# A fused Nyström attention, softplus block and expert layer: w_out blocks decoded in attention, product banks moved, one mixture unit issued in one piece

## The chip, the cores and the metric

The kernel runs on one core of a Trainium2 chip. The metric is the device time of one execution in microseconds (us); the median of three runs stands for a kernel. Engines are called TensorE (PE in the profile, PEld for its weight loads), VectorE (DVE), ScalarE (ACT), GpSimd (POOL) and SyncE (SP, which issues most of the DMAs). TensorE's clock has two levels, 1.2 and 2.4 GHz; the profile shows the granted one as a share of the higher.

## What is computed

Three stages follow one another. `w_in` and `w_out` come in as 64-bit floats, the other inputs and the results are float32.

```python
def _attn_ref(q, k, v):                      # (4, 8, 576, 64) each, 32 landmarks
    A  = sm(q, k_lm); Bm = sm(q_lm, k_lm); C = sm(q_lm, k)
    Z  = Bm.T / (norm1(Bm) * norminf(Bm) + 1e-06)
    for _ in range(6):
        Z = 2 * Z - Z @ Bm @ Z               # pseudo-inverse
    return A @ Z @ C @ v

def _moe_ref(x, w_in, w_out):                # x (2304, 512), w_in (512, 2048), w_out (2048, 512)
    h = x @ w_in
    g = np.maximum(h, 0.0) + np.log1p(np.exp(-np.abs(h)))
    return g @ w_out

def _moe2_ref(x, w_gate, w_output_gate, w1, w2):   # 8 experts, one per token
    ...
```

## The kernel before

Each product in the second and third stage is made of three matmuls on high and low halves: a float32 operand is split into `hi` (rounded) and `lo` (the rest), and hi·hi, hi·lo and lo·hi are added up in a bank of PSUM.

Attention is written as a list of steps, `PLAN`, which a scheduler may interleave on each engine. K, V are loads, T transposes, M landmarks, A and C scores, N the pseudo-inverse (tile tag `sm0`, `sm1` of pool `psm`), E the product with v, F the last product of a batch (tile `ps_x` of pool `pss`, copied by ScalarE to `xo`, line 379). `W i` decodes block i of w_in and `O` decodes block 0 of w_out, while attention runs: a load on SP, `decode_f64` (ScalarE's Abs at line 96, then three VectorE operations at lines 97, 99 and 101 that put the bits together), and `split_hi_lo` (ScalarE copies `hi`, GpSimd subtracts `lo`). The plan has W0 to W9 and one O. `X` prepares the first chunk of x, `x0`.

The mixture (the second stage) goes over 9 chunks of 256 tokens and 8 pairs p of 128-column blocks. One unit is `gemm1(p, x)` (24 matmuls, line 618, into a bank `ps_h`), softplus on ScalarE and VectorE (two halves `gh`, `gl`), and `gemm2` (12 matmuls, line 657, into two banks `acc` of its chunk). Chunks 0 to 2 run jointly, pair by pair, in units 0 to 23, because w_in and w_out are still being decoded; chunks 3 to 8 follow in units 24 to 71. `gemm2` of a unit stands two units behind its `gemm1` (`LAG = 2`). `ps_h` has two banks; units 2 and 3 borrow `acc2` and `tr`. The order on every engine in this stage is the order of the text (`tc.manual_schedule()`).

`weights()` decodes what attention has not: 15 blocks of w_out and 6 of w_in, a list of 21 jobs sorted by when they are due, in four steps each, with VectorE subtracting `lo`. Raw blocks have three buffers, and `load_w(n + 3)` issues a load when block n is decoded. `units(n)` takes n steps. Twelve steps, three jobs, stand ahead of the loop; then each unit takes `U = 1, 1, 2` steps at three places. Softplus of a unit is cut in three pieces, `softplus_a` in its own turn, `softplus_b` and `softplus_c` in the next:

```python
                if i - 1 in ga:
                    gs[i - 1] = softplus_b(*ga.pop(i - 1))
                ...
                    h = gemm1(p, xs[c], *HB.get(i, ()))
                    units(u[0])
                    sp_ = softplus_a(h)
                    next(sp_)
                    if i - 1 in gs:
                        gs[i - 1] = softplus_c(gs[i - 1])
                    ga[i] = next(sp_)
                    units(u[1])
```

`split_x` splits a later chunk's x, at unit 23 for chunk 3. `gate` and `early` make the routing of a finished chunk in small steps (`next(side)`) between the products, two per unit and four in the last chunk (`hook`). The third stage (`run_slots`) keeps the transposed hidden tiles `hh`, `hlo` in pool `e3`, three deep.

Of the kernel before, what the change touches and what calls it, by code (L numbers as in the profile page):

```python
# [1 line left out]

# [27 lines left out]
CH = 256  # L30
# [9 lines left out]
N1 X0 V5 M6 C4 T6 C5 C6 E4 M7 V6 V7 N2 A5 E5 W0 F1 N3 W1 W2 E6 W3 T7 A6 W4 O0 C7 A7 W5 F2 W6 E7 W7 F3 W8 W9  # L40
"""
NWA = 10
# [5 lines left out]
U = 1, 1, 2  # L48
# [38 lines left out]
def decode_f64(nc, pool, src, shape, tag="dect", **kw):  # L87
# [28 lines left out]
def moe_nystrom_kernel(ctx: ExitStack, tc: tile.TileContext, q, k, v, w_in, w_out, w_gate, w_ogate, w1, w2,  # L116
# [23 lines left out]
    wo0 = [x0_pool.tile([128, DM], F32R, name=n) for n in ("wo0h", "wo0l")]  # L140


    with ExitStack() as actx:
# [267 lines left out]
        def prep_wo0():  # L411
            raw = ld.tile([128, 2 * DM], I32, tag="q", name="raw")
            nc.sync.dma_start(raw, w_out.bitcast(I32)[:128, :])
            a = list(decode_f64(nc, a3, raw.unsqueeze(1), [128, 1, DM], bufs=2))[-1]
            split_hi_lo(nc, a[:, 0], wo0[0], wo0[1], nc.gpsimd)
# [12 lines left out]
            "O": lambda _: prep_wo0(),  # L428
# [115 lines left out]
    with ExitStack() as mctx:  # L544
# [9 lines left out]
        woh = [wo0[0]] + [wo.tile([128, DM], F32R, name=f"woh{f}") for f in range(1, NFF)]  # L554
        wol = [wo0[1]] + [wo.tile([128, DM], F32R, name=f"wol{f}") for f in range(1, NFF)]

        due = [(3 * (f // 2) + 2 * (f == 1), "o", f) for f in range(1, NFF)]
# [14 lines left out]
        def weights():  # L572

            for n, (kind, f) in enumerate(jobs):
                for a in decode_f64(nc, m2, raws.pop(n).unsqueeze(1), [128, 1, DM], tag="x2t"):
                    if a is None:
                        yield
                load_w(n + 3)
                yield
                a = a[:, 0]  # L580
                if kind == "o":
                    split_hi_lo(nc, a, woh[f], wol[f], nc.vector)
                else:
                    split_hi_lo(nc, a.rearrange("p (k f) -> p k f", k=4), wcols(whi, f), wcols(wlo, f), nc.vector)
                yield
# [38 lines left out]
        def softplus_a(h):  # L624
            t = sp.tile([128, 2, CH], F32, tag="t", name="t")
            u = sp.tile([128, 2, CH], F32, tag="u", name="u")
            l = sp.tile([128, 2, CH], F32, tag="l", name="l")
            nc.scalar.activation(t, h, AF.Abs)  # L628
            nc.scalar.activation(t, t, AF.Exp, scale=-1.0)  # L629
            nc.scalar.activation(u, t, AF.Identity, bias=1.0)  # L630
            yield
            nc.scalar.activation(l, t, AF.Ln, bias=1.0)  # L632
            nc.vector.scalar_tensor_tensor(u, u, -1.0, t, ALU.add, ALU.subtract)  # L633
            yield h, u, l

        def softplus_b(h, u, l):

            d = sp.tile([128, 2, CH], F32, tag="d", name="d")
            nc.vector.scalar_tensor_tensor(d, h, 0.0, u, ALU.max, ALU.subtract)  # L639
            nc.vector.tensor_tensor(l, l, d, ALU.add)  # L640
            return l

        def softplus_c(l):
            gh = m3.tile([128, 2, CH], F32R, tag="gh", name="gh")
            gl = m3.tile([128, 2, CH], F32R, tag="gl", name="gl")
# [194 lines left out]
        with tc.manual_schedule():  # L840
# [3 lines left out]
            for nm, src in ((0, w_gate), (1, w_ogate)):  # L844
                nc.sync.dma_start(wg[:, :, nm * NE:(nm + 1) * NE], src.rearrange("(k p) e -> p k e", p=128))
# [31 lines left out]
            for i in range(len(order) + LAG):  # L877
# [12 lines left out]
                if i - 1 in ga:  # L890
                    gs[i - 1] = softplus_b(*ga.pop(i - 1))
# [195 lines left out]
```

## Time and profile before

| | |
|---|---|
| median of 3 runs | 920.24 us (918.68 to 920.66) |
| the profiled execution | 920.92 us, of which 919.1 are the span of the trace |
| TensorE busy | 863.8 us, 94% |
| VectorE, ScalarE, GpSimd busy | 72%, 64%, 23% |
| mean granted clock of TensorE | 0.982 |

Attention ends near 150 us, the joint units end near 303, chunks 3 to 8 near 602, and the experts take the rest. A line of a timeline gives the start, the duration, engine, line, operation, the tile written and those read, the count of merged instructions, and in brackets how long the engine stood idle before it and what released it. A line of a table by stage gives, for a stretch, the busy time of each engine with its count of instructions, the granted clock and the share of time in which DMA engines were busy. Busy times of overlapping matmuls merge into one, and the distance of two starts says more than a duration.

### The profile page before, as it was taken

To read this page: it belongs to the slowest core of one execution; us is meant where nothing else is said; L and a number is where in the kernel's file an instruction comes from. 1 tells how busy PE (TensorE), PEld (TensorE's weight loads), DVE (VectorE), ACT (ScalarE), POOL (GpSimd) and SP (SyncE) were. 2 spreads that over 40 slices of the span, in tenths; PEclk is the share of its full clock that TensorE was granted. 3 is DMA by queue.
4 is the path that set the end of the run, shared out by engine and by line. 5 is a ranking of instruction groups with operands and counts; after the bars stand their busy time and mean duration, and the time that the engine had idled before them with its cause. 6 is when DMAs were issued, how large, how long until landed. Compare 5 with 4: busy or idle time off the path is not lost.

```text
span 919.1 us, 15441 instructions
## 1 busy us (share of the span) xinstructions
PE 863.8 (94%) x5826; PEld 717.5 (78%) x5826; DVE 660.8 (72%) x1121; ACT 589.2 (64%) x958; POOL 209.6 (23%) x109
## 2 busy tenths in 40 slices
PE   6998987599999999999999999998999999999996
PEld 3665655478788899999999998886878888888885
DVE  0846697787775546665546464668899999999994
ACT  2554564666666655555555555464888888888893
POOL 0001132000000000000000000024666677666662
PEclk9999997799999999999999999999999999999998
DMA  9856466323210000100111000141117459531600
GB/s 228 188 137 182 146 189 194 94 89 92 82 46 13 24 1 24 46 22 4 46 46 47 1 24 1 47 184 47 44 37 264 174 182 378 184 126 34 225 31 33
DMA packets 49516, 90.93 MB, mean 99 GB/s; under 512 B 5471, under 2 KB 32095, under 8 KB 47392
## 3 DMA queue, kind: packets, MB, share of 16 engines
q1 hardware_dynamic: 41408, 74.43, 26.1%
q0 software_dynamic: 3680, 10.78, 3.6%
q10 hardware_dynamic: 4352, 4.72, 1.5%
q8 instruction: 47, 0.77, 0.4%
q14 instruction: 29, 0.24, 0.1%
HBM read 134.46 MB, written 15.48 MB: 163 GB/s over the span
## 4 chain that ended last, share of the span: by engine, by line
PE 68%; DVE 13%; ACT 10%; issue 4%; DMA 4%; POOL 0%; SPq 0%; POOLq 0%; ACTq 0%; DVEq 0%
PE ps_h L618 16%; PE acc L657 14%; PE ps_g L956 12%; PE ps_y L982 11%; DVE dect L99 2%; DVE deca L101 2%; PE ps_hT L970 2%; PE ps_lg L682 2%; ACT t L629 2%; ACT u L630 2%; ACT deca L96 2%; ACT gh L646 1%; DVE u L633 1%; PE ps_t L184 1%; PE ps_t L160 1%
## 5 line engine op out<-in xcount | busy, mean ns | idle before, releaser
L478 DVE TENSOR_TENSOR lo<-raw,hi 128x1024 fp32r<-128x1024 f32 x129 | 228.7, 1799 | 8.8 <-ACT hi L476 8.6
L476 ACT ACTIVATE hi<-raw 128x1024 fp32r<-128x1024 f32 x176 | 176.8, 1063 | 8.4 <-DMA raw<-in_moe_w 8.3
L618 PE MATMUL ps_h<-xh,whi 128*128 128x256 f32 x512 | 147.4, 288 | 5.8 <-DVE d L639 4.1
L618 PE MATMUL ps_h<-xl,whi 128*128 128x256 f32 x512 | 144.9, 283 | 0.3 <-DVE xl L107 0.3
L618 PE MATMUL ps_h<-xh,wlo 128*128 128x256 f32 x512 | 144.8, 283 | 0.0
L647 DVE TENSOR_TENSOR gl<-l,gh 128x512 fp32r<-128x512 f32 x72 | 49.9, 692 | 129.0 <-ACT gh L646 129.0
L485 POOL DMA_INDIRECT xg<-x_d,gidx x23 | 37.8, 1645 | 452.4 <-ACT t L628 441.4
L478 POOL TENSOR_TENSOR lo<-raw,hi 128x1024 fp32r<-128x1024 f32 x47 | 115.9, 2468 | 35.3 <-ACT hi L476 35.2
L618 PEld LDWEIGHTS ps_h<-xh,whi 128*128 128x128 f32 x512 | 98.0, 191 | 11.4 <-DVE d L639 7.9
L618 PEld LDWEIGHTS ps_h<-xl,whi 128*128 128x128 f32 x512 | 98.0, 191 | 1.9 <-DVE xl L107 0.5
L618 PEld LDWEIGHTS ps_h<-xh,wlo 128*128 128x128 f32 x512 | 97.9, 191 | 0.0
L657 PE MATMUL acc<-woh,gh 128*128 128x512 f32 x240 | 96.2, 401 | 0.0
L657 PE MATMUL acc<-wol,gh 128*128 128x512 f32 x240 | 94.5, 394 | 0.0
L657 PE MATMUL acc<-woh,gl 128*128 128x512 f32 x240 | 94.3, 393 | 0.0
L628 ACT ACTIVATE t<-ps_h 128x512 f32<-128x512 f32 x72 | 42.6, 592 | 69.6 <-PE ps_h L618 50.0
L632 ACT ACTIVATE l<-t 128x512 f32<-128x512 f32 x72 | 45.5, 632 | 55.1 <-DVE gl L647 55.1
L982 PE MATMUL ps_y<-hi,hh 128*128 128x512 f32 x184 | 76.7, 417 | 0.2 <-ACT hh L974 0.2
L982 PE MATMUL ps_y<-hi,hlo 128*128 128x512 f32 x184 | 73.3, 398 | 1.7 <-DVE hlo L975 1.6
L956 PE MATMUL ps_g<-hi,x0l 128*128 128x512 f32 x184 | 73.9, 402 | 0.1
L982 PE MATMUL ps_y<-lo,hh 128*128 128x512 f32 x184 | 72.7, 395 | 0.0
L956 PE MATMUL ps_g<-hi,x0h 128*128 128x512 f32 x184 | 72.0, 391 | 0.0
L956 PE MATMUL ps_g<-lo,x0h 128*128 128x512 f32 x184 | 71.9, 391 | 0.0
(263 smaller groups left out, 1790.4 us busy)
## 6 DMA issues: line engine op xcount, KB each, us to landing
raw<-in_moe_w SPq DMA_DIRECT2D x88, 1024.0 KB
raw<-in_moe_w_in SPq DMA_DIRECT2D x16, 512.0 KB
raw<-in_moe_w_out SPq DMA_DIRECT2D x16, 512.0 KB
x_d<-x SPq DMA_DIRECT2D x9, 514.0 KB
k<-in_k SPq DMA_DIRECT2D x8, 576.0 KB
q<-in_q SPq DMA_DIRECT2D x8, 576.0 KB
v<-in_v SPq DMA_DIRECT2D x8, 576.0 KB
xT_d<-xo ACTq DMA_DIRECT2D x16, 288.0 KB
```

The source lines that it names most:

```text
L96: nc.scalar.activation(a, hi32.bitcast(F32), AF.Abs, scale=2.0 ** -112)
L99: nc.vector.scalar_tensor_tensor(t, hi32, -0x80000000, t, ALU.bitwise_and, ALU.bitwise_or)
L476: nc.scalar.activation(w[0][:, us], raw[i][:, us], AF.Copy)
L478: eng.tensor_tensor(w[1][:, us], raw[i][:, us], w[0][:, us].bitcast(F32), ALU.subtract)
L485: nc.gpsimd.indirect_dma_start(out=xg, out_offset=None, in_=src, in_offset=bass.IndirectOffsetOnAxis(ap=gidx[:, s:s + 1], axis=0))
L618: nc.tensor.matmul(ps[:, i], a[:, kk], b_[:, kk], start=n == 0, stop=n == 11)
L628: nc.scalar.activation(t, h, AF.Abs)
L632: nc.scalar.activation(l, t, AF.Ln, bias=1.0)
L647: nc.vector.tensor_tensor(gl, l, gh.bitcast(F32), ALU.subtract)
L657: nc.tensor.matmul(acc[tt], a[:, i, ts_], b_[f], start=f == 0 and n == 0, stop=f == NFF - 1 and n == 2)
L956: nc.tensor.matmul(ps, a[:, kk], b_[:, kk], start=n == 0, stop=n == 11)
L982: nc.tensor.matmul(y, a[:, kk], b_[:, kk], start=half == 0 and n == 0, stop=half == 1 and n == 11)
```

## The change

`O` becomes a step with an argument: O0, O1 and O2 decode blocks 0 to 2 of w_out in attention, and W8 and W9 are dropped from the plan, so that blocks 8 to 15 of w_in are decoded in the mixture. `units(12)` ahead of the loop is gone; unit 0 takes no weight step inside its softplus. `weights()` works one job ahead: ScalarE's Abs of the next block is issued with the `hi` copy of this one, then `lo`, then the three VectorE operations of the next block; three steps per job, one job per unit, and a further job after units 5 and 8 (`EXTRA`). A unit's softplus is issued in one piece in its own turn. Setting up the routing constants and loading the gate weights moves from ahead of the loop to behind unit 2. Pool `psm` is created ahead of `pss`, so that `ps_h`, which takes the third and fourth bank, lies where `psm` was. In the last stage `hh` and `hlo` cycle through the space of the three w_out blocks.

```diff
-... W5 F2 W6 E7 W7 F3 W8 W9
+... W5 F2 W6 O1 E7 W7 F3 O2
-NWA = 10
+NWA = 8
+NWO = 3
+EXTRA = 0, 5, 8
-U = 1, 1, 2
...
     nc.scalar.activation(a, hi32.bitcast(F32), AF.Abs, scale=2.0 ** -112)
+    yield
     nc.vector.tensor_scalar(t, a.bitcast(I32), 3, None, ALU.logical_shift_left)
-    yield
     nc.vector.scalar_tensor_tensor(t, hi32, -0x80000000, t, ALU.bitwise_and, ALU.bitwise_or)
-    yield
     nc.vector.scalar_tensor_tensor(a.bitcast(I32), lo32, 29, t, ALU.logical_shift_right, ALU.bitwise_or)
...
+        psm = actx.enter_context(tc.tile_pool(name="psm", bufs=1, space=PSUM))
         pss = actx.enter_context(tc.tile_pool(name="pss", bufs=2, space=PSUM))
-        psm = actx.enter_context(tc.tile_pool(name="psm", bufs=1, space=PSUM))
...
-        def prep_wo0():
+        def prep_wo(f):
             raw = ld.tile([128, 2 * DM], I32, tag="q", name="raw")
-            nc.sync.dma_start(raw, w_out.bitcast(I32)[:128, :])
+            nc.sync.dma_start(raw, w_out.bitcast(I32)[f * 128:(f + 1) * 128, :])
...
         def weights():
+            dec = {}
+            def start(n):
+                if n < len(jobs):
+                    dec[n] = decode_f64(nc, m2, raws.pop(n).unsqueeze(1), [128, 1, DM], tag="x2t")
+                    next(dec[n])
+            def finish(n):
+                if n < len(jobs):
+                    dec[n] = next(dec[n])[:, 0]
+                    load_w(n + 3)
+            start(0)
+            finish(0)
+            yield
             for n, (kind, f) in enumerate(jobs):
...
+                nc.scalar.activation(hi, a, AF.Copy)
+                start(n + 1)
                 yield
...
+                nc.vector.tensor_tensor(lo, a, hi.bitcast(F32), ALU.subtract)
+                yield
+                finish(n + 1)
                 yield
...
-        def softplus_a(h):
+        def softplus(h, units):
...
             nc.scalar.activation(t, h, AF.Abs)
             nc.scalar.activation(t, t, AF.Exp, scale=-1.0)
             nc.scalar.activation(u, t, AF.Identity, bias=1.0)
-            yield
             nc.scalar.activation(l, t, AF.Ln, bias=1.0)
+            units(1)
             nc.vector.scalar_tensor_tensor(u, u, -1.0, t, ALU.add, ALU.subtract)
...
             nc.vector.scalar_tensor_tensor(d, h, 0.0, u, ALU.max, ALU.subtract)
             nc.vector.tensor_tensor(l, l, d, ALU.add)
...
             nc.scalar.activation(gh, l, AF.Copy)
+            units(1)
             nc.vector.tensor_tensor(gl, l, gh.bitcast(F32), ALU.subtract)
+            units(1)
             return gh, gl
...
-            units(12)
             for i in range(len(order) + LAG):
...
-                    units(u[0])
...
+                    gs[i] = softplus(h, units if i else int)
+                    if i in EXTRA:
+                        units(1 if i == 0 else 3)
+                    if i == 2:
+                        nc.vector.tensor_copy(tri_b, cc("tri"))
...
+                        for nm, src in ((0, w_gate), (1, w_ogate)):
+                            nc.sync.dma_start(wg[:, :, nm * NE:(nm + 1) * NE], src.rearrange("(k p) e -> p k e", p=128))
...
+        hht = cycle([[wo0[j][f].rearrange("p (k n) -> p k n", k=4) for j in range(2)] for f in range(NWO)])
...
-            hh = e3.tile([128, 4, 128], F32R, tag="hh", name="hh")
-            hlo = e3.tile([128, 4, 128], F32R, tag="hlo", name="hlo")
+            hh, hlo = next(hht)
```

## Rows read from the trace of the kernel before

**Rows 1.** By stage: length, busy PE, PEld, DVE, ACT, POOL, clock, DMA share, GB/s.
```profile
160.00:171.34 11.34, 0.00 (x0) 0.00 (x0) 7.59 (x13) 7.00 (x12) 0.00 (x0) 0.64 0.35 112
171.34:179.57 8.23, 8.23 (x37) 7.03 (x37) 6.25 (x11) 5.22 (x9) 0.00 (x0) 0.67 0.30 102
179.57:275.83 96.26, 90.76 (x550) 77.26 (x549) 76.02 (x124) 62.60 (x107) 0.00 (x0) 1.00 0.25 74
275.83:303.02 27.19, 26.86 (x176) 24.32 (x175) 15.46 (x24) 16.15 (x29) 0.00 (x0) 1.00 0.04 11
```

**Rows 2.** TensorE's timeline (start, duration, what) around the first units.
```profile
149.67 0.58 PE L618 MATMUL ps_h<-x0h,whi 128*128 128x256 f32 x1 [0.37 <-ACT xo L379]
...
153.94 0.28 PE L618 MATMUL ps_h<-x0h,wlo 128*128 128x256 f32 x1
...
159.69 0.28 PE L618 MATMUL ps_h<-xh,wlo 128*128 128x256 f32 x1
171.34 0.79 PE L657 MATMUL acc<-wo0h,gh 128*128 128x512 f32 x1 [11.37 <-ACT gh L646]
...
176.63 0.35 PE L618 MATMUL ps_h<-xh,whi 128*128 128x256 f32 x1
...
179.57 0.40 PE L657 MATMUL acc<-woh,gh 128*128 128x512 f32 x1
...
182.48 0.28 PE L618 MATMUL ps_h<-x0h,whi 128*128 128x256 f32 x1
```

**Rows 3.** ScalarE's timeline: starts of softplus of units 2, 17, 22, 23, 24.
```profile
176.86 0.59 ACT L628 ACTIVATE t<-ps_h 128x512 f32<-128x512 f32 x1
...
270.18 0.58 ACT L628 ACTIVATE t<-ps_h 128x512 f32<-128x512 f32 x1
...
297.40 0.60 ACT L628 ACTIVATE t<-ps_h 128x512 f32<-128x512 f32 x1 [0.81 <-ACT x L666]
...
303.02 0.60 ACT L628 ACTIVATE t<-ps_h 128x512 f32<-128x512 f32 x1 [1.78 <-PE ps_h L618]
...
311.25 0.60 ACT L628 ACTIVATE t<-ps_h 128x512 f32<-128x512 f32 x1 [3.36 <-issue]
```

**Rows 4.** VectorE's timeline: steps of a decode and of softplus.
```profile
173.84 0.42 DVE L97 TENSOR_SCALAR dect<-deca 128x512 int32<-128x512 int32 x1
174.29 0.69 DVE L99 SCALAR_TENSOR_TENSOR dect<-raw,dect 128x512 int32<-128x512 int32 x1
175.02 0.69 DVE L101 SCALAR_TENSOR_TENSOR deca<-raw,dect 128x512 int32<-128x512 int32 x1
...
277.29 0.69 DVE L640 TENSOR_TENSOR l<-l,d 128x512 f32<-128x512 f32 x1
278.68 0.69 DVE L647 TENSOR_TENSOR gl<-l,gh 128x512 fp32r<-128x512 f32 x1 [0.70 <-ACT gh L646]
279.29 0.69 DVE L633 SCALAR_TENSOR_TENSOR u<-u,t 128x512 f32<-128x512 f32 x1
280.08 0.69 DVE L639 SCALAR_TENSOR_TENSOR d<-ps_h,u 128x512 f32<-128x512 f32 x1
```

**Rows 5.** ScalarE's timeline: an x copy, a wait for a load, unit 23.
```profile
151.65 0.62 ACT L106 ACTIVATE xh<-xr 128x512 fp32r<-128x512 f32 x1
...
158.07 0.69 ACT L96 ACTIVATE deca<-raw 128x512 f32<-128x512 f32 x1 [2.54 <-DMA raw<-in_moe_w_out]
...
304.31 0.63 ACT L630 ACTIVATE u<-t 128x512 f32<-128x512 f32 x1
304.85 0.62 ACT L646 ACTIVATE gh<-l 128x512 fp32r<-128x512 f32 x1
...
306.76 1.13 ACT L106 ACTIVATE xh<-xr 128x512 fp32r<-128x512 f32 x2
```

**Rows 6.** SP's timeline: the load that ScalarE waited for in group 5.
```profile
151.56 0.58 SPq L567 DMA_DIRECT2D raw<-in_moe_w_out  x1
```

**Rows 7.** TensorE's waits from 560 to 602 us (total, times, longest).
```profile
PE ps_i L778 <- DVE erhs L773: 1.2, 1, 1.2
PE ps_lg L682 <- ACT x2t L677: 0.3, 1, 0.3
```

More of the change, by code (lines that the diff above doesn't have):

```diff
@@ L1 @@
 from contextlib import ExitStack, nullcontext
+from itertools import cycle
 import numpy as np
@@ L139, in moe_nystrom_kernel @@
     x0 = [x0_pool.tile([128, 4, CH], F32R, name=n) for n in ("x0h", "x0l")]
-    wo0 = [x0_pool.tile([128, DM], F32R, name=n) for n in ("wo0h", "wo0l")]
+    wo0 = [[x0_pool.tile([128, DM], F32R, name=f"{n}{f}") for f in range(NWO)] for n in ("woh", "wol")]
     with ExitStack() as actx:
@@ L553, in moe_nystrom_kernel @@
         pa = pool("pa", 1, space=PSUM)
-        woh = [wo0[0]] + [wo.tile([128, DM], F32R, name=f"woh{f}") for f in range(1, NFF)]
-        wol = [wo0[1]] + [wo.tile([128, DM], F32R, name=f"wol{f}") for f in range(1, NFF)]
-        due = [(3 * (f // 2) + 2 * (f == 1), "o", f) for f in range(1, NFF)]
+        woh = wo0[0] + [wo.tile([128, DM], F32R, name=f"woh{f}") for f in range(NWO, NFF)]
+        wol = wo0[1] + [wo.tile([128, DM], F32R, name=f"wol{f}") for f in range(NWO, NFF)]
+        due = [(3 * (f // 2) + 2 * (f == 1), "o", f) for f in range(NWO, NFF)]
         due += [(3 * (f // 2) - 2, "i", f) for f in range(NWA, NFF)]
@@ L572, in weights @@
         def weights():
-            for n, (kind, f) in enumerate(jobs):
-                for a in decode_f64(nc, m2, raws.pop(n).unsqueeze(1), [128, 1, DM], tag="x2t"):
-                    if a is None:
-                        yield
-                load_w(n + 3)
-                yield
[L580 to L584, printed above, removed]
+            dec = {}
[10 more added lines that the diff above has]
+            yield
+            for n, (kind, f) in enumerate(jobs):
+                if kind == "o":
+                    a, hi, lo = dec.pop(n), woh[f], wol[f]
+                else:
+                    a, hi, lo = dec.pop(n).rearrange("p (k f) -> p k f", k=4), wcols(whi, f), wcols(wlo, f)
+                nc.scalar.activation(hi, a, AF.Copy)
+                start(n + 1)
+                yield
+                nc.vector.tensor_tensor(lo, a, hi.bitcast(F32), ALU.subtract)
+                yield
+                finish(n + 1)
                 yield
@@ L843, in moe_nystrom_kernel @@
             load_w(0)
[L844 to L851 removed]
+            gs, accs = {}, {}
             side = iter(())
@@ L888, in moe_nystrom_kernel @@
                     wk[0] = splits(0, NBASE)
-                u = ((0, 0, 3), (0, 2, 3))[i] if i < 2 else U
-                if i - 1 in ga:
-                    gs[i - 1] = softplus_b(*ga.pop(i - 1))
                 if i < len(order):
@@ L898, in moe_nystrom_kernel @@
                         next(side, None)
-                    units(u[0])
-                    sp_ = softplus_a(h)
-                    next(sp_)
-                    if i - 1 in gs:
-                        gs[i - 1] = softplus_c(gs[i - 1])
-                    ga[i] = next(sp_)
-                    units(u[1])
+                    gs[i] = softplus(h, units if i else int)
[3 more added lines that the diff above has]
+                        nc.vector.tensor_copy(tri_b, cc("tri"))
+                        nc.vector.tensor_copy(one_b, cc("ones"))
+                        nc.vector.memset(osum[:, 0], 0.0)
+                        nc.vector.tensor_copy(sgn[:, 0], cc("iota")[:1, :NE])
+                        nc.vector.tensor_scalar(sgn[:, 1], cc("iota")[:1, :NE], -1.0, None, ALU.mult)
+                        for nm, src in ((0, w_gate), (1, w_ogate)):
+                            nc.sync.dma_start(wg[:, :, nm * NE:(nm + 1) * NE], src.rearrange("(k p) e -> p k e", p=128))
                     if i == nj - 1:
@@ L909, in moe_nystrom_kernel @@
                         xs[c + 1] = split_x(load_xr(c + 1))
-                if i - 1 in gs and i >= len(order):
-                    gs[i - 1] = softplus_c(gs[i - 1])
-                units(u[2])
                 if i >= len(order):
```

23 lines of the change are left out of this document (6 added, 17 removed).

## The prediction

> **What bounds the kernel now.** I read the per-stage table first, then TensorE's timeline where the table shows holes, then the two engines that feed it. The page's total (TensorE 94% busy) hides that the stages have different limits. [rows 1] is the stretch from the end of attention to the end of the joint stage, in four pieces. In the first TensorE does nothing for 11.34 us while VectorE and ScalarE work 7.6 and 7.0 us. In the second its granted clock is still 0.67, a mean over both levels. In the third, 96 us long, nothing is full: TensorE 90.8, VectorE 76.0, ScalarE 62.6. In the fourth TensorE is nearly always busy.
>
> [rows 2] gives the hole its edges. The first product of the mixture (unit 0, 24 matmuls) starts at 149.67 after 0.37 us on the copy of `xo`, its last matmul starts at 153.94, the third unit's last at 159.69, and the first `gemm2` matmul at 171.34, on `gh`. What fills the 11.4 us are the three weight jobs put in front of the loop (`units(12)`): they need w_out block 1 on the chip, and ScalarE stands 2.54 us for it [rows 5], so softplus of unit 0 starts at 164 though its product was ready at 154. After the hole the first `gemm2` takes 176.63 − 171.34 = 5.29 us at the low clock; the next takes 182.48 − 179.57 = 2.91.
>
> The third piece is a chain that goes round between ScalarE and VectorE. Softplus starts are the marks [rows 3]: unit 2 at 176.86 and unit 17 at 270.18, so 93.32 / 15 = 6.22 us per unit; units 22 and 23, without weight jobs, are 5.62 apart. 5.62 is what TensorE needs for one `gemm1` and one `gemm2`: from there on it is full.
>
> How much of the third piece is to be had? The page's busy share of TensorE says 96.26 − 90.76 = 5.5 us. The marks say (6.22 − 5.62) × 15 = 9.0. The Trainium skill ("Perfetto Trace Analysis", Identifying the Most-Contended Engine) says that matmul busy time misleads, since matmuls overlap, and that weight-load busy time should be used. By it: 77.26 busy here, against 24.32 of 27.19 (89%) in the full piece [rows 1], gives 77.26 / 0.894 = 86.4, so 9.9 us. The trace sides with the page: its figure is near that of the marks, and the busy share is too small. The sum below goes by the marks alone.
>
> **The change part by part.** I call P(n) the start of `gemm2` of unit n; P(21) follows the product of unit 23. Before, P(0) = 171.34 and P(21) = 303.02.
>
> Start. With w_out blocks 0 to 2 decoded in attention, softplus of unit 0 waits only for its product. ScalarE finishes the x copies at 151.65 + 0.62 = 152.3 [rows 5], so it begins at 154.1. Steps after the start T [rows 3, 5]: ScalarE's `u` begins at T + 1.29 and ends at T + 1.92, so VectorE begins at T + 1.96. VectorE's steps [rows 4]: u to d 0.79 (I take the same for d to l), l to gl 1.39 (it goes over ScalarE's `gh`). So `gl` begins at T + 4.93 = 159.0 and ends at 159.7; `gemm2`, whose third matmul is the first to need it, can start at 159.8. P(0): 171.34 to 159.8. `ps_h` now lies on banks that the pseudo-inverse left long before, not on those of `ps_x`: the 0.37 us wait goes too, P(0) = 159.4. That is −11.9.
>
> Decoding moved. O1 and O2 take the place of W8 and W9: the same six steps per block on ScalarE, VectorE and POOL, one load each on SP, so I take 0. Bounds: they stand ahead of the last batch's steps rather than behind, and two decodes are 2 × (0.42 + 0.69 + 0.69) = 3.6 us of VectorE [rows 4], so +3.6; below nothing by the same amount, if VectorE's tail gets shorter. Two w_in blocks come into the mixture and two of w_out leave it: 21 jobs either way. The gate weights' loads and five small VectorE copies go behind unit 2; they add about 0.5 us to VectorE there, and SP loses two loads ahead of the raw weights.
>
> Pace. VectorE's new order per unit is u, d, l, lo, gl, then three decode steps of the next block. Steps [rows 4]: u to d 0.79, d to l 0.79, l to gl 1.39 (`lo` fits in that wait), gl to the next 0.61, decode 0.45 and 0.73, and 0.61 to the next u: 5.37 us. The trace has no such order; its bounds are the eight operations back to back, 7 × 0.61 + 0.45 = 4.7, and the old order's 6.22. I take 5.37, being nearest to the steps as they stand. ScalarE's seven operations at 0.54 to 0.66 are about 4.1 us and fit inside. So VectorE falls under 5.62, and TensorE sets the pace: 21 × 5.62 = 118.0 from P(0) to P(21), against 131.7: −13.7. Of that 5.29 − 2.91 = 2.4 is the low clock, since TensorE no longer stands still before the first `gemm2`.
>
> Extra jobs. `EXTRA` runs one more job straight through after units 5 and 8. There ScalarE's hi copy waits for the decode (0.72), VectorE's lo for the copy (0.67), then 0.61 + 0.45 + 0.73: 3.2 us of VectorE each. The margin is 0.1 us at the start (`gl` ready against `gemm2` starting) plus 0.46 up to its third matmul, then 0.25 per unit, less 0.5 for the small copies. So about 1.55 of the first is covered and 0.75 of the second: +1.65 and +2.45, +4.1 together. Bounds 0 and 6.4.
>
> So P(21) = 159.4 + 118.0 + 4.1 = 281.5, from 303.02: −21.5.
>
> Entry of chunk 3. Its x split is queued behind softplus of unit 23. Before, ScalarE's copy came at 306.76, 3.74 us after that unit's start, and unit 24 started at 311.25, 8.23 after [rows 3, 5]. In one go ScalarE first waits for `l` to write `gh`: T + 4.27, and the copy at T + 4.81. So +1.1.
>
> From chunk 3 on nothing else changes while TensorE is full: `gemm2` of a unit starts 11 us after its softplus, which takes 5.7. The last chunk is different. There gate and routing steps stand four to a unit, and TensorE already waits for ScalarE and VectorE at three of them, 1.2, 0.3 and 0.3 us [rows 7] (two of the three are shown). ScalarE's copies for them now come behind `gh`, 1.07 us later as above; I take 0.7 each, +2.1, with bounds 0 and 3 × 1.07 = 3.2. The hidden tiles of the last stage move to the w_out blocks' space, still three deep: 0.
>
> Sum: −21.5 + 1.1 + 2.1 = −18.3. The profiled span of 919.1 becomes 900.8; 1.8 us lie around it, so the profiled execution's 920.9 becomes 902.6. It was 0.7 above the median of the three runs, 920.24, which becomes 901.9.
>
> **The rivals.** *Earlier still.* With `ps_h` on free banks, the products of units 0 and 1 can go into TensorE's waits before 149, and softplus of unit 0 starts when the x copies end, 152.3 instead of 154.1. For it: those products need only x0 and early w_in blocks. Against: the chain then hangs on VectorE, so only that 1.8 us comes through, and perhaps the extra jobs' 2 us: 898.
>
> *The chain stays the bound.* If the new order closes at 5.95 (half way from 5.62 to the old 6.22), TensorE waits every unit: 21 × 0.33 = 6.9 more, and the extra jobs are wholly exposed, 6.4 instead of 4.1: 911. For it: VectorE waits for `gh` inside the unit, and nothing of another unit fills that wait but `lo`. It decides from 5.62, 0.25 above my count.
>
> *Slower: the raw load in ScalarE's queue.* The Abs of block n+1 now stands in ScalarE's order ahead of `gh`, so a late block holds up gh, VectorE's gl, `gemm2` and every later softplus. A load issued at 151.56 released ScalarE at 158.07 [rows 5, 6], 6.5 us. Three buffers leave about 2.7 units, 15 us, from issue to use. If landing took 18.2 us the pace would be 18.2 / 2.7 = 6.74, 23.5 us more than counted: 925. It decides from 15 us, and is slower than before from about 17.5. Against it: DMA is a quarter busy there [rows 1].
>
> *It doesn't do what it says.* Softplus of unit 0 stays behind other work (the attention's last decode, the x copies held up by the moved blocks), and the hole opens again elsewhere: the start's 11.9 and some of the pace are lost and about 919 remains.
>
> **How the numbers follow.** Forecast 0.66 (898 to 906), earlier 0.14, chain 0.13, raw load 0.04, hole stays 0.03. The range takes the first three: below, no extra stalls and no late steps (−4.1 − 2.1) reach 895.7; above, 3.6 more in attention or half the chain's price reach 906 to 910. So 895 to 910. A measurement of this kernel can tell about 0.2%, 1.8 us, from no change: faster 0.93, same 0.02, slower 0.05 (the raw load, and a small rest).
>
> **What would show it.** Right: no hole of more than 1 us between unit 2's product and the first `gemm2`, clock 1.00 there, softplus starts 5.6 apart from unit 3 on, with bumps after units 5 and 8, and unit 23 at 281 to 282. Wrong: marks 5.9 or more apart (the chain), ScalarE's Abs waiting for a DMA (the raw load), or the last `ps_x` later than 148 (the attention pays).

## The result and the profile after

The changed kernel takes 910.29 us (median of 4 runs, 910.17 to 911.31). Beside it the kernel before took 919.83, and the ratio is 0.9901 with an interval of 0.9886 to 0.9915. So it is faster by 9.5 us, about half of the 18.3 that the prediction counted, and the time lies 0.3 us above the range. The profiled execution took 910.2 us, of which 908.4 are its span (before 919.1); the mean granted clock is 0.988 (before 0.982).

I read the traces by one mark for each of the 72 units: the start of its softplus on ScalarE. Of the 10.7 us by which the span is shorter, 10.2 stand at the mark of unit 71 (591.50, before 601.70). They divide in this way:

| stretch | before | after | difference | forecast |
|---|---|---|---|---|
| mark of unit 23 | 303.02 | 281.25 | −21.8 | −21.5 |
| unit 23 to 24, entry of chunk 3 | 8.23 | 10.72 | +2.5 | +1.1 |
| unit 24 to 45 | 129.37 | 129.85 | +0.5 | 0 |
| unit 45 to 47 | 13.38 | 17.10 | +3.7 | 0 |
| unit 47 to 65 | 107.94 | 108.69 | +0.75 | 0 |
| unit 65 to 69, last chunk | 28.52 | 32.65 | +4.1 | +2.1 |

So the joint stage did what the sum said, and a good half of its gain was given back in the 300 us behind it.

**The joint stage.** This is the table by stage of the changed kernel (length, busy PE, PEld, DVE, ACT, POOL, clock, DMA share, GB/s), which answers [rows 1]:

```profile
151.00:171.00 20.00, 18.41 (x112) 15.71 (x112) 16.08 (x30) 15.84 (x29) 0.00 (x0) 0.97 0.46 144
...
182.00:270.50 88.50, 83.89 (x538) 76.00 (x537) 79.53 (x127) 62.97 (x109) 0.00 (x0) 1.00 0.30 90
```

Of the hole of 11.3 us with no matmul 1.59 us are left, and the stretch at a clock of 0.67 is gone. In TensorE's timeline, which answers [rows 2], the first matmul of a `gemm2` comes at 156.96 rather than 171.34. Unit 21's, P(21) of the prediction, comes at 280.99; the sum said 281.5.

```profile
156.96 0.50 PE L670 MATMUL acc<-woh,gh 128*128 128x512 f32 x1 [1.59 <-ACT gh L657]
...
191.27 0.39 PE L635 MATMUL ps_h<-xh,whi 128*128 128x256 f32 x1 [2.44 <-DVE d L655]
...
280.99 0.40 PE L670 MATMUL tr<-woh,gh 128*128 128x512 f32 x1
```

VectorE's timeline of the changed kernel from unit 5 on shows the order that the prediction summed from [rows 4], and then the extra job:

```profile
181.18 0.69 DVE L654 SCALAR_TENSOR_TENSOR u<-u,t 128x512 f32<-128x512 f32 x1
181.97 0.69 DVE L655 SCALAR_TENSOR_TENSOR d<-ps_h,u 128x512 f32<-128x512 f32 x1
182.76 0.69 DVE L656 TENSOR_TENSOR l<-l,d 128x512 f32<-128x512 f32 x1
183.37 0.69 DVE L599 TENSOR_TENSOR wol<-deca,woh 128x512 fp32r<-128x512 f32 x1
184.16 0.69 DVE L659 TENSOR_TENSOR gl<-l,gh 128x512 fp32r<-128x512 f32 x1
184.77 0.42 DVE L100 TENSOR_SCALAR dect<-deca 128x512 int32<-128x512 int32 x1
185.22 0.69 DVE L101 SCALAR_TENSOR_TENSOR dect<-raw,dect 128x512 int32<-128x512 int32 x1
185.95 0.69 DVE L102 SCALAR_TENSOR_TENSOR deca<-raw,dect 128x512 int32<-128x512 int32 x1
187.34 0.69 DVE L599 TENSOR_TENSOR wlo<-deca,whi 128x512 fp32r<-128x512 f32 x1 [0.70 <-ACT whi L596]
...
189.74 0.68 DVE L654 SCALAR_TENSOR_TENSOR u<-u,t 128x512 f32<-128x512 f32 x1
```

From u to the next u it is 189.74 − 181.18 = 8.56 us with the extra job in it, so the extra job is 8.56 − 5.37 = 3.19, if the plain order is 5.37. The marks confirm that: they are 5.37 or 5.38 apart from unit 10 to unit 20, and around the job after unit 5 they are 9.12 and 4.81 apart, 3.19 more than twice 5.37. Before, they were 6.22 apart [rows 3]. TensorE itself goes on at 5.62 a unit between its waits; marks 5.37 apart mean that softplus catches up with products that already lie finished in their banks.

**The entry of chunk 3.** ScalarE's copy of `x` starts at 286.06, which is unit 23's start + 4.81, the figure of the prediction (ScalarE's timeline, changed kernel):

```profile
281.25 0.60 ACT L649 ACTIVATE t<-ps_h 128x512 f32<-128x512 f32 x1 [0.17 <-PE ps_h L635]
...
286.06 1.13 ACT L107 ACTIVATE xh<-xr 128x512 fp32r<-128x512 f32 x2
```

TensorE's waits (us in total, times, longest) from 281 to 293 in the changed kernel:

```profile
PE ps_h L635 <- ACT xh L107: 2.8, 1, 2.8
PE ps_h L635 <- DVE xl L108: 0.4, 1, 0.4
```

Before, the same two were 1.7 and 0.3, so 1.2 us are waits, as forecast. The other 1.3 are the clock. The table by stage of the changed kernel, the wait and what follows it:

```profile
284.00:288.70 4.70, 1.55 (x10) 1.35 (x11) 3.28 (x5) 1.67 (x3) 0.00 (x0) 1.00 0.02 5
288.70:292.70 4.00, 4.00 (x20) 3.82 (x19) 0.00 (x0) 0.70 (x2) 0.00 (x0) 0.57 0.47 126
```

and of the kernel before:

```profile
305.00:309.00 4.00, 1.91 (x11) 1.25 (x11) 2.89 (x5) 2.13 (x4) 0.00 (x0) 1.00 0.00 0
309.00:314.00 5.00, 5.00 (x34) 4.51 (x33) 1.26 (x3) 2.38 (x4) 0.00 (x0) 1.00 0.41 107
```

A granted clock of 0.57 over 4 us is 0.43 × 4 = 1.7 us of TensorE lost, of which the marks show the 1.3: nearly all of the 4 us are at the lower of its two levels, 1.2 GHz.

**Units 45 to 47.** Here a queue that the prediction had not looked at decides. SP's timeline, ahead of chunk 5's start, in the changed kernel:

```profile
422.91 0.36 SPq L751 DMA_DIRECT2D x_d<-x  x1
423.36 2.44 SPq L615 DMA_DIRECT2D xr<-xT_d  x4
```

and in the kernel before:

```profile
439.93 0.36 SPq L738 DMA_DIRECT2D x_d<-x  x1
440.38 2.46 SPq L598 DMA_DIRECT2D xr<-xT_d  x4
```

Against the mark of unit 45 (421.82, before 440.62) the store of `x_d` moved from 0.7 us ahead of it to 1.1 us behind it, and the load of `xr` stands behind the store on SP. The store waits for the gate's steps on VectorE; in the changed kernel they stand behind `gl` of the unit before, as VectorE's timeline shows:

```profile
421.07 0.69 DVE L659 TENSOR_TENSOR gl<-l,gh 128x512 fp32r<-128x512 f32 x1 [0.70 <-ACT gh L657]
421.68 0.48 DVE L746 TENSOR_SCALAR rmat<-cst,rk 128x128 bf16<-128x128 f32 x2
```

The load's lateness then goes on through ScalarE, whose timeline has the copy of `xr` and behind it the copy that the gate's matmul needs:

```profile
428.32 1.15 ACT L107 ACTIVATE xh<-xr 128x512 fp32r<-128x512 f32 x2 [1.60 <-DMA xr<-xT_d]
429.38 0.58 ACT L690 ACTIVATE x2t<-ps_tr 128x512 f32<-128x512 f32 x1
```

TensorE waits 2.5 us for `x2t` (none in that place before), and again the clock falls. The table by stage of the changed kernel:

```profile
430.00:434.00 4.00, 3.99 (x18) 3.37 (x19) 2.51 (x5) 2.22 (x4) 0.00 (x0) 0.76 0.00 0
434.00:439.00 5.00, 5.00 (x36) 4.61 (x35) 0.70 (x2) 1.30 (x3) 0.00 (x0) 0.85 0.01 3
```

That is 0.24 × 4 + 0.15 × 5 = 1.7 us of clock beside the 2.5 of waiting, 4.2, of which the marks show 3.7.

**The last chunk.** TensorE's waits from 546 to 592 in the changed kernel, which answer [rows 7]:

```profile
PE ps_n L767 <- DVE cd L736: 1.8, 1, 1.8
PE ps_tr L689 <- ACT x L679: 1.4, 1, 1.4
PE ps_lg L695 <- ACT x2t L690: 1.4, 1, 1.4
```

They sum to 4.6, against 1.8 before (1.2, 0.3, 0.3). The clock takes its part here too (table by stage, changed kernel; both pieces stood at 1.00 before):

```profile
558.00:564.00 6.00, 4.64 (x27) 4.08 (x26) 3.36 (x11) 1.11 (x2) 0.00 (x0) 0.82 0.00 0
564.00:570.00 6.00, 6.00 (x37) 5.33 (x37) 1.61 (x3) 2.38 (x4) 0.00 (x0) 0.90 0.00 0
```

### The profile page after: what moved, and what is told of

It is laid out like the page before. It is cut to its first block, busy times and chain, and to the rows that moved or that the text cites. A ratio compares the mean times of both kernels' runs of the same rounds, so it can differ in the third digit from the quotient of the medians.

```text
span 908.4 us, 15419 instructions
## 1 busy us (share of the span) xinstructions
PE 859.9 (95%) x5826; PEld 718.9 (79%) x5826; DVE 666.5 (73%) x1121; ACT 586.9 (65%) x958; POOL 209.5 (23%) x109
## 4 chain that ended last, share of the span: by engine, by line
PE 68%; DVE 14%; DMA 6%; ACT 6%; issue 4%; POOL 0%; SPq 0%; DVEq 0%; POOLq 0%; ACTq 0%
PE ps_h L635 19%; PE acc L670 15%; PE ps_g L960 10%; PE ps_y L985 9%; DMA raw<-in_moe_w 3%; DVE lo L479 2%; DVE dect L101 2%; PE ps_hT L974 2%; ACT hi L477 2%; PE ps_lg L695 2%; DVE deca L102 1%; PE ps_t L185 1%; PE ps_t L161 1%; DVE l L656 1%; DVE d L655 1%
## 5 line engine op out<-in xcount | busy, mean ns | idle before, releaser
L479 DVE TENSOR_TENSOR lo<-raw,hi 128x1024 fp32r<-128x1024 f32 x129 | 226.3, 1781 | 11.4 <-ACT hi L477 11.1
L657 ACT ACTIVATE gh<-l 128x512 fp32r<-128x512 f32 x72 | 45.5, 632 | 116.0 <-DVE l L656 116.0
L654 DVE SCALAR_TENSOR_TENSOR u<-u,t 128x512 f32<-128x512 f32 x72 | 49.6, 688 | 83.5 <-ACT u L651 83.4
L670 PE MATMUL acc<-woh,gh 128*128 128x512 f32 x256 | 103.1, 403 | 1.6 <-ACT gh L657 1.6
L670 PE MATMUL acc<-wol,gh 128*128 128x512 f32 x256 | 101.0, 394 | 0.0
L670 PE MATMUL acc<-woh,gl 128*128 128x512 f32 x256 | 100.8, 394 | 0.0
L985 PE MATMUL ps_y<-hi,woh 128*128 128x512 f32 x184 | 76.7, 417 | 0.2 <-ACT woh L977 0.2
L985 PE MATMUL ps_y<-hi,wol 128*128 128x512 f32 x184 | 73.3, 398 | 1.4 <-DVE wol L978 1.3
L985 PE MATMUL ps_y<-lo,woh 128*128 128x512 f32 x184 | 72.7, 395 | 0.0
```

The costliest lines, as they stand in the source:

```text
L479: eng.tensor_tensor(w[1][:, us], raw[i][:, us], w[0][:, us].bitcast(F32), ALU.subtract)
L670: nc.tensor.matmul(acc[tt], a[:, i, ts_], b_[f], start=f == 0 and n == 0, stop=f == NFF - 1 and n == 2)
L985: nc.tensor.matmul(y, a[:, kk], b_[:, kk], start=half == 0 and n == 0, stop=half == 1 and n == 11)
```

## The experiments

Theory: in the joint stage the one-piece softplus gains what was counted, but from unit 24 on it puts other work (copies of `x`, gate steps, and through them a store and a load) behind `gh` and `gl`, and TensorE waits for that at three places, each time with some low clock after it. Rivals: the loss is at the entry alone; it comes from the new banks; the extra jobs cost more than counted; or the hole alone was the gain and the rest of the change brings nothing. The kernel before stood at 919.3, 918.3 and 919.1 beside the three sets (e1 to e4, e5 to e8, e9 to e11).

| kernel | median (us) | ratio to before |
|---|---|---|
| after | 910.29 | 0.9901 (0.9886 to 0.9915) |
| e1_start_only | 916.83 | 0.9981 (0.9967 to 0.9994) |
| e2_cut_from_24 | 903.36 | 0.9823 (0.9802 to 0.9843) |
| e3_split_early | 906.34 | 0.9844 (0.9824 to 0.9864) |
| e4_xr_ahead | 908.69 | 0.9882 (0.9866 to 0.9899) |
| e5_banks_back | 911.39 | 0.9908 (0.9880 to 0.9936) |
| e6_one_extra | 909.41 | 0.9891 (0.9866 to 0.9916) |
| e7_both_ahead | 902.58 | 0.9822 (0.9794 to 0.9850) |
| e8_all | 896.99 | 0.9759 (0.9735 to 0.9783) |
| e9_all_three_jobs | 896.12 | 0.9751 (0.9724 to 0.9779) |
| e10_extra_late | 910.54 | 0.9901 (0.9874 to 0.9927) |
| e11_all_late | 896.65 | 0.9747 (0.9721 to 0.9773) |

The intervals of e4, e5, e6 and e10 overlap that of the changed kernel, so what they show is read from the marks and waits, not from the medians. Even with the same instructions the profiled executions differ: unit 0's mark lies between 150.78 and 152.37 in the kernels that share the changed kernel's attention, and what follows unit 71 takes 316.9 to 319.7 us.

**e1_start_only**: the kernel before with the three w_out blocks decoded in attention and no jobs ahead of the loop; softplus and the weight jobs keep their old order.

```diff
-... W5 F2 W6 E7 W7 F3 W8 W9
+... W5 F2 W6 O1 E7 W7 F3 O2
-            units(12)
```

> The kernel before with one part of the change: w_out blocks 0 to 2 decoded in attention in place of two w_in blocks, and no weight jobs ahead of the loop; softplus cut in three pieces, the weight steps, the banks and the order of everything else as before (the hidden tiles take the w_out blocks' space). My theory: this alone closes the hole of 11.4 us and its low clock (2.4), but the three jobs that stood ahead now run in the loop, where a unit with a job takes 6.22 us, so that unit 23 comes at about 294 against 303.0 before and 281.3 after: 911 to 912 us, about what the whole change gives. Rival: most of the gain is in the pace of the joint stage, so this alone gives under 4 us: 917 or more.

It gained 2.4 us, so the expectation missed; the rival (under 4 us, 917 or more) came within 0.2. The start did come earlier: unit 0's mark is 152.82 (before 164.41) and unit 17's 258.51 (before 270.18), 11.6 and 11.7 less. But units 3 to 18 are still 6.2 apart, and the jobs that the hole had done now come as units 18 to 20; unit 19 even comes 9.08 after unit 18, since TensorE stands 3.13 us for `whi` of a late block. At unit 23 only 6.2 are left. Removing the hole is worth little while the units behind it are slower than TensorE: the work in the hole comes back at their pace. The other 15.6 of the 21.8 come with the rest of the change, the new pace above all; what the new pace gives while the hole stays was not run.

Another 1.5 of the 6.2 go at the entry, and it is instructive: unit 24 comes 9.75 after unit 23, not 8.23, though the order is the old one and TensorE's waits in e1 are the same as before to a tenth:

```profile
PE ps_h L620 <- ACT xh L108: 1.7, 1, 1.7
PE ps_h L620 <- DVE xl L109: 0.3, 1, 0.3
```

What differs is the clock behind them, 1.00 before and lower here (table by stage, e1):

```profile
300.00:304.00 4.00, 2.42 (x11) 2.22 (x11) 3.19 (x6) 1.67 (x3) 0.00 (x0) 0.76 0.18 45
304.00:308.00 4.00, 4.00 (x23) 3.70 (x23) 0.00 (x0) 1.36 (x3) 0.00 (x0) 0.82 0.32 86
```

So low clock worth 1.5 us by the marks can follow a pair of waits that costs nothing but itself in another kernel.

**e2_cut_from_24**: the changed kernel, but from unit 24 on softplus is issued in three pieces again, each in the turn of another unit.

```diff
-                    gs[i] = softplus(h, units if i else int)
+                    if i < 24:
+                        gs[i] = softplus(h, units if i else int)
+                    else:
+                        sp_ = softplus_a(h)
+                        next(sp_)
+                        if i - 1 in gb:
+                            gs[i - 1] = softplus_c(gb.pop(i - 1))
+                        ga[i] = next(sp_)
```

> The changed kernel, with softplus in one piece only in units 0 to 23; from unit 24 on it is cut in three pieces as before. My theory: issuing softplus in one piece is what loses 9 us behind unit 24 (units 24 to 45 0.5, units 45 to 47 3.7, units 47 to 65 0.7, the last chunk 4.1), because gate copies and x copies queue behind gh, and gate steps of VectorE behind gl. So 910.3 falls to about 901 to 902, and the marks from 24 on have the distances of before. Rival: the loss lies in what comes early (chunk 3's entry, transfers that meet other work when everything is 20 us sooner), and the cut changes under 2 us: 908 or more.

903.36: 6.9 us less than the changed kernel, most of the 8 to 9 that the theory said and far from its rival. The waits of the last chunk are those of before (e2, 540 to 586):

```profile
PE ps_i L816 <- DVE erhs L811: 1.2, 1, 1.2
PE ps_lg L720 <- ACT x2t L715: 0.3, 1, 0.3
PE ps_tr L714 <- ACT x L704: 0.3, 1, 0.3
```

Units 65 to 69 take 28.53 again (before 28.52), and units 46 and 47 come after 6.98 and 7.47 (after: 8.03 and 9.07). The entry is untouched by the edit (unit 23 is still in one piece) and stays at 10.89. From the mark of unit 24 to that of unit 71 it is 290.45 before, 299.53 in the changed kernel and 291.50 in e2. So the one-piece softplus is the cause of 8.0 of the 9.1 us lost behind unit 24, and the rival "entry alone" falls. The last 1.1 stay at units 45 to 47 (14.45, before 13.38): the store of `x_d` is back at 0.7 us ahead of unit 45's mark, but the load behind it, issued at 421.95, releases ScalarE only at 427.63, after 5.68 us (before 4.65). Why that load took longer stays open.

**e3_split_early** and **e4_xr_ahead** move a load and its split instead. In e3 the `x` of chunk 3 is loaded two units and split one unit earlier; in e4 the load of every later chunk is issued three units earlier, so ahead of the store on SP.

```diff
-                    if i == nj - 1:
+                    if i == nj - 3:
                         xr.append(load_xr(JOINT))
...
-                    if i == nj - 1:
+                    if i == nj - 2:
                         xs[JOINT] = split_x(xr.pop(0))
```

> The changed kernel, with chunk 3's x loaded behind unit 20 and split behind softplus of unit 22 instead of unit 23. My theory: TensorE's wait of 2.8 and 0.4 us at unit 24, and with it the low clock that follows (about 1.4 to 1.8 us), go: unit 24 starts 5.6 to 5.8 us after unit 23 instead of 10.7, and the time falls by about 5, to 905. Rival (the wait alone costs, the low clock is its own matter): 3.2 us and the clock still falls, 907. Or the split only holds up softplus of unit 23 instead and under 1 us comes through.

```diff
+                    if p == 2 and JOINT - 1 < c < NCH - 1:
+                        xr.append(load_xr(c + 1))
                     if p == 5 and JOINT - 1 < c < NCH - 1:
-                        xs[c + 1] = split_x(load_xr(c + 1))
+                        xs[c + 1] = split_x(xr.pop(0))
```

> The changed kernel, with the load of a later chunk's x issued at pair 2 of the chunk before instead of pair 5, ahead of the store of the gated chunk in SP's queue; the split stays where it is. My theory: the 3.7 us lost at units 45 to 47 go, because there the store waits for VectorE's gate steps behind gl, the load for the store, ScalarE for the load (1.6 us), and the transposed copy of the gate behind that: TensorE's wait of 2.5 us at the logits and the low clock after it vanish. 906 to 907 us, distances of units 46 and 47 near 6.1 and 7.0. Rival: the copy was late because of gh alone; then the wait shrinks by 1 us at most and the time is 909.

e3 gave 906.34. The copy of `x` now stands ahead of unit 23's softplus, TensorE has no wait from 270 to 300, the clock stays at 1.00, and unit 24 comes 4.82 after unit 23 rather than 10.72: that is 5.9 less. Unit 23 itself, now behind the copy, comes 5.86 after unit 22 rather than 5.09, so from unit 22 on the wait and the low clock gone together are worth 5.1. Some of it is given back at units 45 to 47, where unit 47 takes 10.51 (9.07 in the changed kernel), with 2.6 us of waiting and the clock at 0.50 behind it:

```profile
425.00:430.00 5.00, 5.00 (x14) 4.09 (x15) 2.85 (x5) 1.79 (x4) 0.00 (x0) 0.50 0.00 0
```

e4 gave 908.69, 1.6 less than the changed kernel, where the theory had 3 to 4; the medians are too near to tell. In its own place it did what was expected: units 46 and 47 come after 6.33 and 7.47, 3.3 less together. The wait for `x2t` shrinks from 2.5 to 0.8, and the clock stays up (e4, tables by stage):

```profile
430.00:434.00 4.00, 4.00 (x24) 3.46 (x25) 2.50 (x5) 2.21 (x5) 0.00 (x0) 1.00 0.00 0
434.00:439.00 5.00, 5.00 (x36) 4.65 (x36) 1.30 (x3) 2.58 (x5) 0.00 (x0) 1.00 0.01 3
```

That shows the place of SP's order: the store is still late, only the load no longer stands behind it. The span is only 1.9 shorter: unit 0 already starts 0.8 later in this execution, the entry takes 0.2 more and what follows unit 71 0.7 more, none of it a place of the edit. Counted from unit 0 to unit 71, e4 takes 3.35 less than the changed kernel. Behind the wait of the first extra job the clock falls to 0.91 and 0.66 in two pieces of 4 us here, and yet units 0 to 23 take the same 129.7 as in the changed kernel (129.6), where it stays up; e10, below, shows why.

**e5_banks_back** puts the two pools of banks back in their old order, and **e6_one_extra** drops the job after unit 8.

```diff
+        psm = actx.enter_context(tc.tile_pool(name="psm", bufs=1, space=PSUM))
         pss = actx.enter_context(tc.tile_pool(name="pss", bufs=2, space=PSUM))
-        psm = actx.enter_context(tc.tile_pool(name="psm", bufs=1, space=PSUM))
```

> The changed kernel with the two bank pools in their old order, so that the products of the mixture lie on the banks of the x copies again and the pseudo-inverse's banks go to the smaller tiles. After: 910.3, softplus of unit 0 at 151.61. Theory (the banks are what lets the products of units 0 and 1 be computed before the last x copy): softplus of unit 0 goes back to about 154, as the prediction had counted it, P(0) from 158.6 to about 159.5 to 160, unit 23 at 282 to 283.5; time 911 to 913. Rival A (the banks bring nothing, the pace takes it back): 910.3, unit 23 at 281 to 281.5. Rival B (they matter more than counted, since the last products wait for x copies in turn): 915 and over.

```diff
-EXTRA = 0, 5, 8
+EXTRA = 0, 5
```

> The changed kernel without the extra weight job after unit 8, so that one fewer is run straight through inside the joint stage and the last jobs are one unit later. Theory (each such job puts 3.2 us of VectorE into the chain, of which TensorE sees 2.4): units 8 to 9 come 5.6 to 5.7 apart instead of 9.1 from softplus to softplus, unit 23 at 278.8 to 279.4 instead of 281.25, time 907.5 to 908.5. Rival (the late last blocks are waited for in place of it): unit 23 unchanged, 910.3 or more, with a wait of TensorE or ScalarE on the last blocks near unit 19 to 22.

e5 gave 911.39, 1.1 more than the changed kernel and inside the overlap of the two intervals: no gain of the banks can be told. The product of unit 0 starts at 147.50, again with 0.38 us on the copy of `xo` (in the changed kernel it is pulled forward to 136.41), and softplus of unit 0 starts at 152.13, not at 154. Before, that product started at 149.67 [rows 2], so about 2 us of the earlier start come from a shorter attention: the moved decodes seem to help there, though executions with one and the same attention differ by 1.6. Unit 23 comes at 281.46, 0.2 later than in the changed kernel, so next to nothing is left of the earlier product by then.

e6 gave 909.41, within its spread of the changed kernel; the rival held. TensorE's waits from 155 to 290 in e6:

```profile
PE ps_h L635 <- DVE d L655: 2.7, 2, 2.4
PE ps_h L635 <- DVE wlo L599: 1.6, 1, 1.6
...
PE ps_h L635 <- ACT whi L596: 0.3, 1, 0.3
```

One of the two long waits for the release by `d` is gone (after: 4.8 in three, the long ones 2.44 and 2.17), and 1.6 and 0.3 for the late weights come in its place: units 19 and 20 come after 7.09 and 7.14, and unit 23 comes 1.5 later than in the changed kernel. The extra job pays for itself.

**e7_both_ahead** has the edits of e3 and e4 together, **e8_all** has those of e2, e3, e4 and e6, and **e9_all_three_jobs** is e8 with the third job back.

> The changed kernel with both loads of x ahead: chunk 3's loaded three units before the end of the joint stage and split one unit earlier, and in every later chunk the load issued before the gate steps rather than behind the store that waits for them. Alone the first gave 906.3 and the second 908.7, against 910.3 for the changed kernel. Theory (two separate places, so the gains add: entry of chunk 3 about 5, units 45 to 47 about 3.3, less what the last chunk takes back): units 45 to 47 6.0 to 6.4 and 7.4 to 7.6 apart, unit 71 at 583 to 586, time 902.5 to 905. Rival (both pushes only shift the later waits, since the last chunk's gate steps then meet another order): 906 to 907.

> Every place in one kernel: the changed kernel, with softplus in three pieces again from unit 24 on, both loads of x ahead, and one extra weight job fewer. Softplus in pieces alone gave 903.4. Theory (in pieces the later chunks stand as before the change; the entry of chunk 3 gives up to 5 to 9 more as its wait and the low clock after it go, the extra job 2.4): 893 to 897, unit 24 4.8 to 5.7 after unit 23. Rival (the entry's gain was a matter of the order of one-piece softplus and is paid back later, as it was in part at unit 47 when chunk 3 alone was split early): 899 to 901.

> The kernel with every place mended (softplus in three pieces from unit 24 on, both loads of x ahead) with the three extra weight jobs of the changed kernel instead of two. With two it gave 897.0. Leaving the third out saved one TensorE wait of 2.4 us and brought one of 1.6 and one of 0.3 for the last blocks instead, units 18 to 20 7.0 to 7.2 apart. Theory (the job left out is paid back by the late blocks): 896 to 898, no difference that can be told. Rival (units 18 to 20 cost more than the waits show, since unit 23 came 1.5 later there): 895 to 895.7.

e7 gave 902.58, 7.7 less than the changed kernel. By the medians that is more than the 3.9 and 1.6 of its two halves, but counted from unit 0 to unit 71 the gains add: 7.2 less against 3.8 (e3) and 3.4 (e4). Units 46 and 47 come after 6.33 and 7.46, as in e4. e8 gave 896.99: units 45 to 47 and 65 to 69 as before the change, and the entry 5.23. e9 gave 896.12 and cannot be told from e8, as the theory of the paid-back job said. Both are faster than the kernel before and than the changed one, and with 21 to 23 us they go beyond what the prediction had hoped for, since the entry now costs 4.81 where before it cost 8.23. In e9 TensorE's waits from 280 to 560 are two of 0.3 us and no more.

**e10_extra_late** is the changed kernel with the third job after unit 15 instead of 8, **e11_all_late** is e9 with the same.

```diff
-EXTRA = 0, 5, 8
+EXTRA = 0, 5, 15
```

> The changed kernel with its third extra weight job after unit 15 rather than after unit 8. After: 910.3. Theory (the margin grows by 5.62 less 5.37 = 0.25 us a unit while VectorE is the shorter chain, so that ten units after the job of unit 5 it covers 2.5 of the 3.2 us): TensorE's waits for the bank release go from 4.8 to about 3 us, softplus of unit 16 still 9.1 after that of unit 15, unit 23 at 279.3 to 281.3, time 908 to 909.5. Rival (no margin gathers, the waits stay at 2.4 each): 910.3 and waits of 4.8. Rival (the blocks come late again from unit 14 on): more waits on the weights' lo copies, 910.5 and over.

> Every place mended and the third extra weight job after unit 15. Theory: as with the job after unit 8, less 1 to 1.8 us: 894 to 895.5. Rival (nothing gathers): the same as with the job after unit 8.

The waits shrank, the time did not. In e10 TensorE's waits for `d` are 2.7, not 4.8: the job after unit 15 is covered wholly. But the time is 910.54. The first job's wait, 2.44 us as in the changed kernel, is followed by low clock here (table by stage, e10):

```profile
186.00:190.00 4.00, 2.31 (x11) 1.56 (x9) 3.13 (x6) 3.79 (x7) 0.00 (x0) 1.00 0.32 131
190.00:194.00 4.00, 3.25 (x18) 3.25 (x19) 3.73 (x7) 3.16 (x7) 0.00 (x0) 0.71 0.44 135
194.00:198.00 4.00, 4.00 (x21) 3.52 (x20) 3.69 (x6) 2.77 (x5) 0.00 (x0) 0.86 0.43 130
```

and not there (changed kernel):

```profile
190.00:194.00 4.00, 2.73 (x22) 2.73 (x23) 3.66 (x7) 3.18 (x7) 0.00 (x0) 1.00 0.45 135
194.00:198.00 4.00, 4.00 (x25) 3.51 (x24) 3.74 (x6) 2.78 (x6) 0.00 (x0) 1.00 0.38 111
```

0.29 × 4 + 0.14 × 4 = 1.7 us; in TensorE's timeline the product behind the wait takes 4.47 us up to the next `gemm2` rather than 2.98, 1.5 more. This loss is also cover. VectorE goes on while TensorE is slow, so its margin grows by 1.5 on top of the 0.25 a unit, and that is why nothing of the later job is left to wait for, where the expectation, by the margin alone, had left about 0.7. At the entry TensorE arrives 1.5 us earlier (`gemm2` of unit 21 at 279.51), but the copy of `x` hangs on unit 23's softplus, which comes only 0.75 earlier, so the wait for it grows from 2.8 to 3.5. At unit 24 e10 is 0.6 ahead, and 0.5 of that stood already at unit 0.

e11, 896.65, cannot be told from e9 by its median. Low clock does not set the two apart: it falls to 0.83 and 0.74 in e11 and just as far in e9 (stretch, busy PE, clock, DMA share, GB/s of e9):

```profile
190.00:194.00 4.00, 3.54 (x20) 0.67 0.43 135
194.00:198.00 4.00, 4.00 (x21) 0.91 0.43 131
```

So in e9 the second job's wait had already shrunk, and its waits for `d` are 3.3 in all; in e11 they are 2.7, and only 0.6 was to be had. Counted from unit 0 to unit 71 e11 takes 0.9 less.

## Why the prediction was right and wrong

- **Start: right, with one reason that did not matter.** The first `gemm2` comes at 156.96 where the sum had 159.4. The rival *Earlier still* came true in its mechanism: the products of units 0 and 1 went into TensorE's waits before the last x copies. It did not come true in the time, because the earlier start is used up by TensorE's waits for `d` of units 6 and 9. A sign that the prediction had named for an attention that pays, a last `ps_x` later than 148, did come (150.97), and yet unit 0's softplus began at 151.61, 2.5 earlier than summed: with the products pulled ahead, that sign meant nothing. The banks, which the step credited with 0.37 us, are worth nothing that e5 could measure.
- **Decoding moved: the value 0 was perhaps a little too careful.** e1 and e5, which have the move without the banks, start the first product at 147.93 and 147.50 instead of 149.67. That lies within the bounds, and is little more than executions differ by.
- **Pace: right.** 5.37 us of VectorE's order was measured as 5.37. *The chain stays the bound* is ruled out by that. That the hole alone carries little of the joint stage's gain is what e1 shows: with the hole gone and the old pace, 6.2 of 21.8 are left at unit 23.
- **Extra jobs: right in size, with the cover otherwise spread.** 3.19 us each against 3.2; TensorE's waits are 4.8 in all against 4.1 counted, 2.44 and 2.17 of them for the two jobs. The margin of 0.25 a unit shows in the second: 2.17 of 3.19 are left after three units, so 1.0 was covered where 0.75 was counted. e10 does not test it, since low clock adds to the margin there. What the prediction did not ask is what the job saves: without the third, 1.9 of waits for late blocks stand in its place (e6).
- **P(21): right, partly by luck.** 280.99 against 281.5, but P(0) came 2.4 earlier than summed, and from there to P(21) it took 124.0 us instead of 122.1. The two misses nearly cancel.
- **Entry of chunk 3: mechanism right, size off.** The copy came at T + 4.81, and the waits grew by 1.2 as counted. But the term was 2.5, not 1.1: it left out the low clock behind the longer wait, 1.3 of the 2.5. The prediction had used the very same effect at the start of the mixture, where it took 2.4 us off, and did not ask for it in a wait that grows.
- **"From chunk 3 on nothing else changes while TensorE is full": this step failed.** Its argument was about `gemm2` alone, which has 11 us for a softplus of 5.7. But the one-piece softplus also sets when everything issued behind it begins. The gate's steps on VectorE came behind `gl`, the store of `x_d` on SP behind the gate, the load of `xr` behind the store, the copies of `xr` and `x2t` on ScalarE behind the load, and the gate's matmul behind those: 2.5 us of waiting and 1.7 of low clock at units 45 to 47, 3.7 by the marks. e4 shows that link in SP's order, e2 shows the cause (it gives back all but 1.1 of the loss behind unit 24). The Trainium skill ("Perfetto Trace Analysis", Tensor Engine Instruction (MATMUL, LD_WEIGHTS)) says that ScalarE, VectorE and GpSimd take their instructions strictly in order, while TensorE can pull weight loads ahead. The trace agrees for VectorE: the gate's steps start at 421.68, 0.61 after `gl` at 421.07 and never ahead of it, though `gl` itself stood 0.70 us for `gh`. Smaller losses, 0.5 and 0.75, lie in the other chunks. e2 takes them away too (129.34 and 107.94), but of them only 0.4 us show as a wait of TensorE, for ScalarE's copy `x`.
- **Last chunk: mechanism right, size off.** Three late copies were counted at 0.7 each and at most 1.07. Two of TensorE's waits grew from 0.3 to 1.4, as much as the upper bound each; a new one of 1.8 on VectorE's `cd` replaced the 1.2 on `erhs`, and then the clock fell: 0.18 × 6 + 0.10 × 6 = 1.7. Together 2.8 + 1.7 = 4.5, of which the marks show 4.1.

The gap between the forecast and the measured time is 910.3 − 901.9 = 8.4. By the marks it is 3.7 (units 45 to 47) + 1.4 (entry) + 2.0 (last chunk) + 1.25 (the other chunks) − 0.3 = 8.05. The other two rivals found nothing in the trace: no Abs of ScalarE waits for a load in the joint stage, and the hole did not open again elsewhere there.

What decides whether the clock falls after a wait of 2 to 2.5 us stays open.

## What to carry to other kernels

An edit of an order is not confined to the stage for which it is made: if the same order runs on where TensorE is full, list every instruction queued behind the moved ones on each engine, and follow each through the DMA queue that it feeds, not only to the matmul that reads its result. A load behind a store on one queue inherits the store's wait (3.3 us at units 45 to 47, e4). Where an edit lengthens a wait of TensorE, the low clock that may follow it (1.3 to 2.7 us here) belongs into the sum as a case of its own, with a chance, and with the question whether another engine's chain hides it.

## What the runs showed of the hardware that was not expected

A wait of TensorE does not have one price. In the changed kernel three waits are followed by some 1.7 us lost to the lower clock each (granted 0.57 over 4 us, 0.76 and 0.85 over 9, 0.82 and 0.90 over 12), and in e3 a wait of 2.6 us by 0.50 and 0.96 over 10 us, 2.7 lost. A wait of the same length does not always bring it: 1.7 + 0.3 us at the entry left the clock at 1.00 in the kernel before and was followed by 0.76 and 0.82 in e1. The 2.4 us behind the first extra job left it at 1.00 over the next 8 us in the changed kernel, e6 and e8, and in the eight other kernels with that job it fell to between 0.66 and 0.91. No run here shows what decides between the two.

Nor does the low clock always cost what it takes. Where VectorE's chain sets the pace, TensorE's next wait shrinks by as much: in e2, e4 and e5 the clock falls behind the first job's wait, the waits for `d` are 3.3, 3.3 and 3.1 us in all instead of 4.8, and units 0 to 23 take 129.6, 129.7 and 129.3 against 129.6. Where TensorE is full it comes on top: removing 3.2 us of waiting and the low clock behind it gave 5.1 at the entry (e3).
